# The first part of the last weight, loaded as 112 + 8 + 8 partitions instead of 128

## The chip, the cores and the metric

The kernel runs on one core of one Trainium2 chip. The metric is the device time of one execution in microseconds (us), median over several runs on the same chip. A core has 16 DMA engines that bring data from the far memory (HBM) into 128 partitions of on-chip memory (SBUF). The repeated runs quoted here are all fast: none took over 1.5% more than the fastest run of its kernel.

## The reference, cut to what matters

One decoding step: attention of one token over a cache of 65,536 keys and values in four heads, plus a small mixer network, added together.

```python
x = A_x
xn = _layernorm(x)
return x + _A_ref(xn, A_k_cache, A_v_cache, A_wq, A_wo) + _B_ref(xn, B_w1, B_w2, B_w3, B_w4)
# in _B_ref, the last product, on which the change bears:
h2 = _gelu(_layernorm(x1) @ w3) @ w4        # w4: 3584 x 1024, bf16, 7.3 MB
```

About 170 MB are read for one token, so the kernel is a long stream of loads with a little arithmetic beside it.

## The kernel before

The cache passes through three slots of 64 KB per partition. The last weight, `w4`, is the last thing to be loaded. It has 28 column blocks of 1,024 values per partition and comes in four parts of falling size, so that little tensor work is left when the last part lands. Every part is one transfer over 128 partitions. A partition's piece of the first part is one run of 17 x 2,048 = 34,816 bytes. I call such a piece of one partition a row below. In the code `P` is 128 and `D` is 1,024; `KV` holds the slots, `q_sp` is the queue of the sync engine, and `chan` gives each transfer its semaphore, a counter that tells when data have landed.

```python
def rows_src(w, r0, nrow):
    return w.rearrange("(p r) n -> p (r n)", p=P)[:, r0 * w.shape[1]:(r0 + nrow) * w.shape[1]]
# ...
w4_parts = [(0, 17), (17, 7), (24, 3), (27, 1)]
b_W4 = [_B() for _ in w4_parts]

def w4_dma(i):
    r0, nr = w4_parts[i]
    _dma(q_sp, chan("w4%d" % i), lambda e: e.dma_start(out=KV[:, slot(20), r0 * D:(r0 + nr) * D], in_=rows_src(B_w4, r0, nr)), writes=[b_W4[i]])
# ... in the last pass over the cache, once the last keys have been read out of that slot:
for i in range(len(w4_parts)):
    # (waits for the readers of the slot: cut)
    w4_dma(i)
# ... at the end, one group of matmuls for each part, as it lands:
for i, (r0, nr) in enumerate(w4_parts):
    out_rows([(gh_bf[:, r:r + 1], KV[:, slot(20), r * D:(r + 1) * D]) for r in range(r0, r0 + nr)], [b_W4[i], b_gh], last=(i == len(w4_parts) - 1))
```

## Time and profile before

The median was 401.73 us (401.70 to 402.13).

| what | before |
|---|---|
| span of the profiled run | 400.7 us |
| rate of all DMA engines, mean | 425 GB/s |
| issue of the last weight | 369.5 us |
| last landing of the last weight | 397.8 us |
| one 34,816-byte row on one engine | 1.29 us |

These lines of the page cut the span into 40 slices of 10 us: first the busy share of the 16 DMA engines in tenths, then what they moved.

```profile
DMA  9999899999999999999999999999999999999994
GB/s 419 419 391 486 381 478 445 420 425 419 432 419 446 464 420 425 419 445 419 440 458 420 419 419 458 427 433 445 428 419 419 446 445 414 445 440 432 393 417 195
```

The engines are full (8 or 9 tenths in every slice) up to the last slice at 390 us.

The timeline has the matmuls of the four parts and the final cast: start, busy time, what it is, and in brackets the idle time just before and who ended it.

```profile
391.04 2.03 PE L543 MATMUL S_ps<-KV,gh_bf 128*1 128x256 bf16 x68 [2.74 <-DMA KV<-in_B_w_dram]
395.29 0.93 PE L543 MATMUL S_ps<-KV,gh_bf 128*1 128x256 bf16 x28 [2.22 <-DMA KV<-in_B_w_dram]
397.18 0.81 PE L543 MATMUL S_ps<-KV,gh_bf 128*1 128x256 bf16 x12 [0.96 <-DMA KV<-in_B_w_dram]
398.16 0.38 PE L543 MATMUL S_ps<-KV,gh_bf 128*1 128x256 bf16 x4 [0.16 <-PE S_ps L543]
398.59 0.43 DVE L612 CAST orow<-S_ps 128x256 bf16<-128x256 f32 x1 [15.77 <-PE S_ps L543]
```

Each part's matmuls wait for its landing. The chain of work that ended last says the same for the end as a whole: start, length, what.

```profile
370.37 26.78 DMA KV<-in_B_w_dram
397.18 0.84 PE S_ps L543 x12
```

The page's list of transfers has size and time from issue to landing:

```profile
KV<-in_B_w_dram SPq DMA_DIRECT2D x1, 4352.0 KB, 21.5
KV<-in_B_w_dram SPq DMA_DIRECT2D x1, 1792.0 KB, 25.4
```

The 21.5 us of the first part is mostly queueing: its first row starts at 377.0 us, behind the load ahead of it.

One thing more is read from the trace's own records. It has 16 updates of the semaphore for each part. I take each for the landing of one engine's share, so that they show how far the engines are apart. For the last part they come in three sets: seven engines at 394.6 to 395.3 us, four at 396.3 to 396.5, and five at 397.6 to 397.8. The packet records show how they drift apart. 13 packets of 16,384 bytes are on the queue that the page calls "q8 instruction"; I call them instruction fetches. Each took 1.02 to 1.11 us, and at the end of twelve of them a packet of the stream starts that takes about 0.5 us longer than others of its size (1.79 us instead of 1.29 for the row after the fetch at 381.1 us). The landings of a load spread as the fetches add up: before the first fetch all 16 come within 0.7 us, after one fetch (load landing from 48.2 us on) one of them is 1.9 us behind the first, after nine (338.7 us) nine are 1.5 to 3.2 us behind.

### The profile page before, as it was taken

How to read it: one execution, taken by the hardware profiler on the slowest of the kernel's cores; microseconds unless marked ns; L12 is line 12 of the kernel's file. 1: busy time of each engine (PE TensorE's matmuls, PEld its weight loads, DVE VectorE, ACT ScalarE, POOL GpSimd, SP SyncE). 2: the span in 40 equal slices, each digit the busy share in tenths (PEclk: the TensorE clock that was granted, in tenths of full speed). 3: DMA queues.
4: the chain of work that ended last, by engine and by line, in shares of the span. 5: the costliest groups of instructions: out<-in, count | busy, mean ns of one | idle time of the engine just before them, and what ended most of it. 6: DMA issues, size and time to landing. Idle time of an engine off the chain costs nothing.

```text
span 400.7 us, 3966 instructions
## 1 busy us (share of the span) xinstructions
PE 176.5 (44%) x1611; PEld 70.7 (18%) x1627; DVE 224.5 (56%) x347; ACT 25.2 (6%) x53; POOL 7.1 (2%) x30
## 2 busy tenths in 40 slices
PE   0034767245334513374345342643462335437664
PEld 0022435011011101121111120111121111102242
DVE  0024221985398446763985558659746685696400
ACT  1000000011001100101011001100110011010100
POOL 5000000000000000000000000000000000000000
PEclk9999668556655655555556656555566656555588
DMA  9999899999999999999999999999999999999994
GB/s 419 419 391 486 381 478 445 420 425 419 432 419 446 464 420 425 419 445 419 440 458 420 419 419 458 427 433 445 428 419 419 446 445 414 445 440 432 393 417 195
DMA packets 3770, 170.13 MB, mean 425 GB/s; under 512 B 548, under 2 KB 552, under 8 KB 808
## 3 DMA queue, kind: packets, MB, share of 16 engines
q1 hardware_dynamic: 3608, 169.87, 98.4%
q8 instruction: 13, 0.21, 0.2%
q14 instruction: 5, 0.04, 0.0%
q10 hardware_dynamic: 144, 0.00, 0.0%
HBM read 169.87 MB, written 0.00 MB: 424 GB/s over the span
## 4 chain that ended last, share of the span: by engine, by line
DMA 41%; DVE 30%; PE 23%; issue 3%; another core or an unknown queue 2%; POOL 0%; SPq 0%; ACT 0%; DVEq 0%
DMA KV<-in_A_k_cache_dram 29%; DVE KV L436 21%; PE S_ps L448 8%; DMA KV<-in_B_w_dram 7%; DMA KV<-in_A_x_dram 6%; PE OT_ps L492 5%; PE S_ps L385 3%; DVE pT_f L483 2%; PE M_ps L400 2%; DVE mrow L455 2%; PE S_ps L353 1%; PE M_ps L520 1%; DVE Yall L369 1%; PE PT_ps L479 1%
## 5 line engine op out<-in xcount | busy, mean ns | idle before, releaser
L436 DVE STREAM_TRANSPOSE KV<-KV 128x1024 f32<-128x1024 f32 x128 | 148.6, 1210 | 8.8 <-DMA KV<-in_A_k_cache_dram 8.7
L448 PE MATMUL S_ps<-KV,Yall 128*32 128x512 bf16 x512 | 60.7, 622 | 114.5 <-DVE KV L436 114.5
L492 PE MATMUL OT_ps<-KV,pT_f 128*32 128x512 bf16 x512 | 59.3, 612 | 1.3 <-PE OT_ps L492 1.3
L448 PEld LDWEIGHTS S_ps<-KV,Yall 128*32 128x32 bf16 x512 | 16.8, 125 | 148.0 <-DVE KV L436 132.2
L483 DVE STREAM_TRANSPOSE pT_f<-PT_ps 128x512 f32<-128x512 f32 x32 | 22.6, 706 | 28.2 <-PE S_ps L448 12.0
L470 ACT ACTIVATE p_sb<-S_ps,brun 128x1024 bf16<-128x1024 f32 x16 | 17.8, 1115 | 281.0 <-DVE brun L468 177.3
L455 DVE TENSOR_REDUCE mrow<-S_ps 128x1 f32<-128x1024 f32 x16 | 19.5, 1216 | 16.8 <-PE S_ps L448 16.7
L479 PE MATMUL PT_ps<-p_sb,permR 128*128 128x512 bf16 x16 | 8.8, 553 | 37.2 <-DVE pT_f L483 37.2
L492 PEld LDWEIGHTS OT_ps<-KV,pT_f 128*32 128x32 bf16 x512 | 17.1, 132 | 35.0 <-issue 33.3
L505 DVE SCALAR_TENSOR_TENSOR O_acc<-O_acc,ff,OT_ps 128x512 f32<-128x512 f32 x12 | 8.9, 744 | 23.6 <-PE OT_ps L492 23.6
L385 PE MATMUL S_ps<-KV 128*32 128x512 bf16 x88 | 12.3, 549 | 2.9 <-DVE KV L333 2.9
L458 PE MATMUL M_ps<-Rm,Lmat 128*128 128x16 bf16 x16 | 3.1, 192 | 22.6 <-DVE Rm L456 22.5
L313 DVE CAST KV<-KV 128x8 f32<-128x8 bf16 x1 | 0.2, 171 | 22.3 <-DMA KV<-in_A_x_dram 22.3
L479 PEld LDWEIGHTS PT_ps<-p_sb,permR 128*128 128x128 bf16 x32 | 3.3, 102 | 43.1 <-ACT p_sb L470 15.4
L612 DVE CAST orow<-S_ps 128x256 bf16<-128x256 f32 x1 | 0.4, 426 | 15.8 <-PE S_ps L543 15.8
L400 PE MATMUL M_ps<-ident_f,pT_f 64*128 64x2 f32 (+2 forms) x32 | 7.9, 373 | 2.3 <-DVE pT_f L393 2.3
L400 PEld LDWEIGHTS M_ps<-ident_f,pT_f 64*128 64x128 f32 (+2 forms) x32 | 7.7, 326 | 4.3 <-DVE pT_f L393 4.3
L393 DVE COPY pT_f<-S_ps 64x512 f32<-64x512 f32 (+1 forms) x3 | 2.1, 686 | 11.1 <-PE S_ps L385 11.1
L523 DVE TENSOR_TENSOR cb_R<-M_ps,maskD 32x128 f32<-32x128 f32 x4 | 1.1, 287 | 12.1 <-PE M_ps L520 12.1
L458 PEld LDWEIGHTS M_ps<-Rm,Lmat 128*128 128x128 bf16 x16 | 1.6, 102 | 34.5 <-DVE Rm L456 34.5
L338 PE MATMUL M_ps<-KV 8*128 8x8 bf16 x1 | 0.2, 161 | 16.2 <-DVE Dmat_f L337 16.2
L543 PE MATMUL S_ps<-KV,gh_bf 128*1 128x256 bf16 x112 | 4.2, 290 | 6.1 <-DMA KV<-in_B_w_dram 5.9
(82 smaller groups left out, 95.4 us busy)
## 6 DMA issues: line engine op xcount, KB each, us to landing
KV<-in_B_w_dram SPq DMA_DIRECT2D x1, 7168.0 KB, 48.1
KV<-in_B_w_dram SPq DMA_DIRECT2D x1, 4352.0 KB, 21.5
KV<-in_B_w_dram SPq DMA_DIRECT2D x2, 2048.0 KB, 28.3
KV<-in_B_w_dram SPq DMA_DIRECT2D x1, 1792.0 KB, 25.4
KV<-in_B_w_dram SPq DMA_DIRECT2D x1, 768.0 KB, 26.8
KV<-in_B_w_dram SPq DMA_DIRECT2D x1, 256.0 KB, 27.0
KV<-in_A_k_cache_dram SPq DMA_DIRECT2D x8, 38.9
KV<-in_A_v_cache_dram SPq DMA_DIRECT2D x8, 29.8
```

Source lines behind the costliest of these rows:

```text
L385: fns.append(lambda e, j=j, k=k, mv=mv: e.matmul(S_ps[32 * (k % 4):32 * (k % 4) + 32, bank + k // 4, :], vec[:, j:j + 1].broadcast_to([P, ...
L400: fns.append(lambda e, b=b, nb=nb, c=c: e.matmul(M_ps[:, c0 + 16 * b + c:c0 + 16 * b + 4 * nb:4], pT_f[0:32 * nb, b, c:512:4], ident_f[0:3 ...
L436: _op(q_dve, lambda e, o=o: e.transpose(out=KV32[:, s, o:o + 1024], in_=KV32[:, s, o:o + 1024]), reads=[b_KV[s][4 * sub + ix]], writes=[b_ ...
L448: fns.append(lambda e, we=we, cm=cm, mv=mv: e.matmul(S_ps[32 * cm:32 * cm + 32, n % 4, :], Yall[:, h, we, :, :].rearrange("p a g -> p (a g ...
L455: _op(q_dve, lambda e: e.reduce_max(mrow[:, k:k + 1], S_ps[:, 2 * k:2 * k + 2, :].rearrange("p b c -> p (b c)"), axis=AX.X), reads=b_S[2 * ...
L458: _op(q_pe, lambda e: e.matmul(M_ps[:, 0:16], Lmat[:, :], Rm[:, k, :], start=True, stop=True), reads=[b_R[k], b_const], writes=[b_M])
L470: _op(q_act, lambda e: e.activation(p_sb[:, :, :].rearrange("p b c -> p (b c)"), S_ps[:, 2 * k:2 * k + 2, :].rearrange("p b c -> p (b c)") ...
L479: _op(q_pe, lambda e: e.matmul(PT_ps[:, :], permR[:, :], p_sb[:, n % 2, :], start=True, stop=True), reads=[b_p[n % 2], b_const], writes=[b ...
L483: _op(q_dve, lambda e: e.transpose(out=pT_f[:, n % 2, :], in_=PT_ps[:, :]), reads=[b_PT], writes=[b_pT[n % 2]])
L492: fns.append(lambda e, q=q, q4=q4: e.matmul(OT_ps[32 * q4:32 * q4 + 32, g % 2, :], pT_bf[:, n % 2, q, :, 1], KV[:, s, 8192 * sub + 512 * q ...
L505: _op(q_dve, lambda e: e.scalar_tensor_tensor(out=O_acc[:, 0:512], in0=O_acc[:, 0:512], scalar=ff[:, k:k + 1], in1=OT_ps[:, k, :], op0=ALU ...
L543: fns.append(lambda e, lhs=lhs, rhs=rhs, jj=jj: e.matmul(S_ps[32 * jj:32 * jj + 1, 0, 0:256], lhs, rhs[:, 256 * jj:256 * jj + 256], start= ...
```

## The change

It means to use that difference: give the engines that end early more rows, and the others fewer. The first part is split by partition. 112 partitions are shared out among all 16 engines, seven rows each; two transfers of 8 partitions run on eight engines, one row each. No record numbers the engines. I call the eight that carry a load of 8 partitions engines 0 to 7, and take them to be the same eight for every such load. So eight engines carry nine rows and eight carry seven, where all carried eight.

```diff
         w4_parts = [(0, 17), (17, 7), (24, 3), (27, 1)]
-        b_W4 = [_B() for _ in w4_parts]
+
+        def w4_split(i):
+            return ((0, 112), (112, 120), (120, P)) if i == 0 else ((0, P),)
+
+        b_W4 = [[_B() for _ in w4_split(i)] for i in range(len(w4_parts))]
 
         def w4_dma(i):
             r0, nr = w4_parts[i]
-            _dma(q_sp, chan("w4%d" % i), lambda e: e.dma_start(out=KV[:, slot(20), r0 * D:(r0 + nr) * D], in_=rows_src(B_w4, r0, nr)), writes=[b_W4[i]])
+            for j, (p0, p1) in enumerate(w4_split(i)):
+                _dma(q_sp, chan("w4%d%d" % (i, j)), lambda e, p0=p0, p1=p1: e.dma_start(out=KV[p0:p1, slot(20), r0 * D:(r0 + nr) * D], in_=rows_src(B_w4, r0, nr)[p0:p1]),
+                     writes=[b_W4[i][j]])
# (cut: the two places that wait for a part now wait for all its transfers)
```

The instructions of the tensor, vector, scalar and pool engines stay the same and in the same order; only the sync queue issues two more transfers.

More of the change, by code (lines that the diff above doesn't have):

```diff
@@ L588, in bass_parallel_sum__gqa_block_cached__mixer_s_mlp__decode_kernel @@
                         for sv, vv in list(bk.r.items()) + list(bk.w.items()):
-                            b_W4[i].add_read((sv, vv))
+                            for bw in b_W4[i]:
+                                bw.add_read((sv, vv))
                     w4_dma(i)
@@ L610, in bass_parallel_sum__gqa_block_cached__mixer_s_mlp__decode_kernel @@
         for i, (r0, nr) in enumerate(w4_parts):
-            out_rows([(gh_bf[:, r:r + 1], KV[:, slot(20), r * D:(r + 1) * D]) for r in range(r0, r0 + nr)], [b_W4[i], b_gh], last=(i == len(w4_parts) - 1))
+            out_rows([(gh_bf[:, r:r + 1], KV[:, slot(20), r * D:(r + 1) * D]) for r in range(r0, r0 + nr)], b_W4[i] + [b_gh], last=(i == len(w4_parts) - 1))
         _op(q_dve, lambda e: e.tensor_copy(orow[:, :], OUT), reads=[b_OUT], writes=[b_orow])
```

## The prediction

The cuts take out what no trace showed: how rows are given to engines, and where engines meet when they write. With them go terms of the forecast's sum, which came to +8 to +11 us by a hand model. The +7.7 us in it is an estimate from the measured 1.29 us of a row: four engines that write neighbouring rows were taken to need 4 x 1.29 = 5.2 us, which is 3.9 us more for each of the two 8-partition transfers. This was an assumption, and it is what the 70% is given to. The two humps of the distribution were put near 402 us without it and near 410 to 412 us with it.

> What bounds the kernel. The page's profile shows the 16 DMA engines busy in tenths of 9 in nearly every slice and 425 GB/s over a 400.7 us span, so the kernel is a stream of transfers. At the end (timeline view) the tensor engine has finished everything else at about 388.3 us and only waits for the last weight: matmuls on its four parts start at 391.0, 395.3, 397.2 and 398.2 us. The chain of waits ends with 26.8 us of that weight's transfer, then 0.84 + 0.41 us of matmuls, a 0.43 us cast and the output store. So the end moves one for one with the last landing, at 397.8 us.
>
> How the tail runs. In the trace's packet records a 34,816-byte row of the first part takes 1.29 us (27 GB/s); each engine carries eight of these rows, then 8 x 0.54, 8 x 0.24 and 8 x 0.08 us. The semaphore updates of the last part come in three groups: seven engines at 394.6 to 395.3 us, four at 396.3 to 396.5, five at 397.6 to 397.8. The late ones are engines that were held up earlier by 16 KB instruction fetches: the packet records show a gap of about 1.05 us and about 0.5 us added to the next packet each time. The intent is visible: give engines with slack more rows.
>
> What changes. [...] So eight engines carry nine rows and eight carry seven, +-1.29 us. Two extra issues on the sync queue (0.43 us each, at about 370 us) are hidden: the part's packets start only at 377 us. Matmul, vector and scalar work is unchanged.
>
> If that were all: nine of 16 engines are not early, so not all can sit among the eight relieved. The end then moves by about -0.1 us (a middle engine gains a row) to +1.3 us (a late one does).
>
> What I expect beside it. [...] My estimate from 1.29 us: [...] +7.7 us on engines with nine rows, on top of the added row, less up to 1-2 us of slack; the 112-row transfer, seven consecutive rows per engine, may collide a little too. [...] I give it about 70%.
>
> Predicted: 409.5 us, range 401.3 to 413.5; faster by over 2% 0.01, within 2% 0.45, slower by over 2% 0.54. The distribution has two humps[...].
>
> What would show it. Right: 34,816-byte packets of the two 8-partition transfers lasting 3 to 5 us instead of 1.29; first part landing 8 or more us later; DMA GB/s falling in the last slices; the other eight engines landing early; the wait of the tensor engine on the last weight growing by the same amount; everything before 377 us unchanged. If the packets stay at 1.29 us, [...] only the one-row shift remains. Also wrong if the 112-partition transfer uses another distribution of rows[...].

## More of the kernel before

The next view has the busy time of each engine in stretches near the end; its last two columns are the DMA engines' busy share and GB/s.

```profile
core 0: us, PE busy (x) PEld busy (x) DVE busy (x) ACT busy (x) POOL busy (x), PEclk, DMA share, GB/s
370.00:380.00 10.00, 6.49 (x112) 2.68 (x105) 4.47 (x11) 1.30 (x3) 0.00 (x0) 0.52 0.94 406
380.00:390.00 10.00, 6.58 (x138) 4.76 (x138) 1.29 (x5) 0.00 (x0) 0.00 (x0) 0.83 0.97 413
390.00:400.00 10.00, 4.15 (x112) 2.44 (x112) 0.43 (x1) 0.00 (x0) 0.00 (x0) 0.84 0.56 228
```

## The result, and the profile after

The median was 419.5 us (418.66 to 420.48), against 401.76 us on the same chip: 1.044 times as long, 95% interval 1.0416 to 1.0465. A ratio here is the mean time of one kernel's fast runs over that of the other's of the same rounds, so it is not quite the ratio of the medians.

The page's slices of the changed kernel, 10.5 us each here:

```profile
DMA  9999899999999999999999999999999999999983
GB/s 400 400 488 438 377 489 406 406 483 406 413 477 406 419 471 406 425 464 401 438 463 396 444 450 403 450 438 409 456 426 419 446 425 431 439 413 230 179 147 155
```

The engines look just as busy, but in the last four slices they move 147 to 230 GB/s. An engine can be busy and move little: a row took 2.3 to 4.6 us instead of 1.29 (medians, below). The stretches of time, in the same columns as before:

```profile
370.00:380.00 10.00, 6.49 (x112) 2.53 (x105) 4.55 (x11) 1.29 (x3) 0.00 (x0) 0.55 1.08 371
380.00:390.00 10.00, 4.97 (x137) 3.72 (x136) 1.29 (x5) 0.00 (x0) 0.00 (x0) 1.00 0.94 214
390.00:400.00 10.00, 0.00 (x0) 0.00 (x0) 0.00 (x0) 0.00 (x0) 0.00 (x0) 0.63 1.12 173
400.00:410.00 10.00, 0.00 (x0) 0.00 (x0) 0.00 (x0) 0.00 (x0) 0.00 (x0) 0.50 0.78 174
```

From 380 us on, with the transfers of the first part under way, the rate is about half or less of the 413 GB/s before. From 390 to 410 us no compute engine does anything. The timeline's tail, the chain and the transfers:

```profile
410.33 3.36 PE L549 MATMUL S_ps<-KV,gh_bf 128*1 128x256 bf16 x68 [20.83 <-DMA KV<-in_B_w_dram]
414.17 0.94 PE L549 MATMUL S_ps<-KV,gh_bf 128*1 128x256 bf16 x28 [0.48 <-DMA KV<-in_B_w_dram]
416.06 0.50 PE L549 MATMUL S_ps<-KV,gh_bf 128*1 128x256 bf16 x12 [0.96 <-DMA KV<-in_B_w_dram]
416.73 0.28 PE L549 MATMUL S_ps<-KV,gh_bf 128*1 128x256 bf16 x4 [0.16 <-DMA KV<-in_B_w_dram]
```

```profile
371.57 45.09 DMA KV<-in_B_w_dram
416.73 0.31 PE S_ps L549 x4
```

```profile
KV<-in_B_w_dram SPq DMA_DIRECT2D x1, 3808.0 KB, 35.7
KV<-in_B_w_dram SPq DMA_DIRECT2D x1, 1792.0 KB, 43.4
```

The tensor engine's idle time before the first part went from 2.74 to 20.83 us, and the end moved with the last landing, from 397.8 to 416.7 us. The 112-partition transfer alone, with 7/8 of the bytes, now takes 35.7 us from issue to landing instead of 21.5.

The trace's packet records say where in the part it happens. They list each row with its start and length; here are the medians of every sixteen rows of the first part, in order of start, in us:

```
before   1.29  1.30  1.29  1.29  1.29  1.30  1.29  1.29
after    2.64  2.46  2.36  2.56  2.32  2.55  4.02  4.58
```

Two things are wrong at once. The 112-partition rows are all nearly twice as slow, from the first on: no row of the first part took under 1.96 us. The rows of the 8-partition transfers, which fall mostly into the last two figures, take three times as long and more.

### The profile page after: what moved, and what is told of

The parts are those of the page before. It is cut to its first block, busy times and chain, and to the rows that moved or that the text cites. A ratio compares the mean times of both kernels' runs of the same rounds, so it can differ in the third digit from the quotient of the medians.

```text
span 419.2 us, 3969 instructions
## 1 busy us (share of the span) xinstructions
PE 175.0 (42%) x1611; PEld 69.9 (17%) x1627; DVE 224.5 (54%) x347; ACT 25.2 (6%) x53; POOL 7.1 (2%) x30
## 4 chain that ended last, share of the span: by engine, by line
DMA 44%; DVE 29%; PE 22%; issue 3%; another core or an unknown queue 2%; SPq 0%; POOL 0%; ACT 0%; DVEq 0%
DMA KV<-in_A_k_cache_dram 28%; DVE KV L436 20%; DMA KV<-in_B_w_dram 11%; PE S_ps L448 8%; DMA KV<-in_A_x_dram 5%; PE OT_ps L492 5%; PE S_ps L385 3%; DVE pT_f L483 2%; PE M_ps L400 2%; DVE mrow L455 1%; PE S_ps L353 1%; PE M_ps L520 1%; DVE Yall L369 1%; DVE pT_f L393 0%
## 5 line engine op out<-in xcount | busy, mean ns | idle before, releaser
L549 PE MATMUL S_ps<-KV,gh_bf 128*1 128x256 bf16 x112 | 5.1, 339 | 22.4 <-DMA KV<-in_B_w_dram 22.4
L549 PEld LDWEIGHTS S_ps<-KV,gh_bf 128*1 128x1 bf16 x112 | 2.9, 102 | 24.7 <-issue 21.1
## 6 DMA issues: line engine op xcount, KB each, us to landing
KV<-in_B_w_dram SPq DMA_DIRECT2D x1, 3808.0 KB, 35.7
```

What stands on the lines that cost most here:

```text
L549: fns.append(lambda e, lhs=lhs, rhs=rhs, jj=jj: e.matmul(S_ps[32 * jj:32 * jj + 1, 0, 0:256], lhs, rhs[:, 256 * jj:256 * jj + 256], start= ...
```

## The experiments

The theories were these. **S**: engines that write rows of one group at the same time slow each other. What a group is, is assumption: four neighbouring rows and the four that lie 32 further on, so 0 to 3 with 32 to 35, and 64 to 67 with 96 to 99. Not every group was tested; these loads of 64 KB rows bear it out, each given with its whole time. In the second kernel of isolated loads (lines 631 and 639 to 642 of its sync queue) rows 0 and 4 took 5.0 us and the eight rows 0, 4, ... 28 took 5.1, but rows 0 and 1 took 6.6, rows 0 and 32 took 7.5, and rows 0 to 3 took 11.2. In the third (line 629) ten rows at a step of 12, no two of one group, took 5.3. **U**: the uneven share, nine rows against seven, is the cost. **H**: the reading side is the cost. **N**: a row is slow if another engine writes it than in the 128-partition form. Three more came up on the way. **C**: an engine that is slowed in a shared group also holds back engines that share none. **K**: something that only 16 engines together meet. **X**: a general limit for engines that write other rows than those of the 128-partition form.

In the recorded expectations, too, the passages on where engines meet are cut. The time that stands right behind a cut at the end of two of them, 9.0 and 419.5 us, is for the case that S plays no part.

### All engines even again, the odd transfers kept

```diff
-            return ((0, 112), (112, 120), (120, P)) if i == 0 else ((0, P),)
+            return ((0, 112), (112, P)) if i == 0 else ((0, P),)
```

> The changed kernel with its two transfers of 8 partitions made one of 16 partitions, so that all 16 engines carry eight rows again, as before. Theory U (the uneven share, nine rows against seven, is the cost): the time goes back to about 402 us. Theory S[...]: the 112-row transfer keeps its 2.45 us a row, which costs 7 x 1.16 = 8.1 us over before; the 16 rows [...] 5.2 us instead of 1.29, so 3.9 us more: about 402 + 12 = 414 us, between 411 and 416.

It took 417.87 us, 1.040 times before. With eight rows on every engine again the loss is nearly all still there, so U falls as the main cause. S had said 411 to 416, so it is too small as sized. The tensor engine's wait for the first part stays nearly as long as in the changed kernel (20.83 us):

```profile
407.67 3.80 PE L549 MATMUL S_ps<-KV,gh_bf 128*1 128x256 bf16 x68 [17.81 <-DMA KV<-in_B_w_dram]
```

### Isolated loads of 34,816-byte rows

Lines were added behind the end of the kernel before. Each waits for the one ahead:

```diff
         q_sp.wait(ev_out)
+        for q in (q_pe, q_dve, q_act, q_pool):
+            q_sp.wait((q.sem, q.cnt))
+        WP = B_w4.rearrange("(p r) n -> p (r n)", p=P)
+        def probe(fn):
+            q_sp.wait(_dma(q_sp, chan("probe"), fn))
+        N = 17 * D
+        probe(lambda e: e.dma_start(out=KV[0:128, 0, 0:N], in_=WP[0:128, 0:N]))
+        probe(lambda e: e.dma_start(out=KV[0:112, 0, 0:N], in_=WP[0:112, 0:N]))
# ... fifteen more
```

> The kernel before with 17 isolated loads added after its output; each waits for the one ahead, a row is 34,816 bytes. The order: 128 rows; 112 from row 0; 112 from row 16; 96; 64; 32; 16; 16 rows at a step of 4; 16 at a step of 8; 16 at a step of 7; 8 rows 112 to 119; 8 at a step of 4 from row 0; the same from row 64; 4 neighbouring rows; 4 at a step of 4; rows 112 to 119 filled from source rows 0, 4, ... 28; rows 0, 4, ... 28 filled from source rows 112 to 119. Theory S[...]: a row takes 1.29 us[...] (128 rows; 8 at a step of 4, from 0 and from 64; 4 at a step of 4), 5.2 us for 4, 8 or 16 neighbouring rows[...], 2.6 us for 16 at steps of 4 and 8, 1.3 to 2.6 at a step of 7; the last two go by the destination: 5.2, then 1.29 us. Theory H (neighbouring source rows collide in the far memory): the last two go by the source. Theory N[...]: 8 rows at a step of 4 are fast from row 0 but slow from row 64. For 112 rows S with seven neighbouring rows per engine expects 10 to 13 us in all; the changed kernel's trace had about 2.45 us a row, so I expect about 17 us unless the rest of the program plays a part.

The timeline of the sync queue for this kernel: start of an issue, its length, source line. As each waits for the one ahead, the distance between two starts is the whole time of a load. Lines 625, 626 and 627 are 128 rows, 112, and 112 from row 16; 635, 636 and 637 are rows 112 to 119, 8 rows at a step of 4 from row 0, and the same from 64; 640 and 641 are the two with exchanged sources.

```profile
400.83 0.34 SPq L625 DMA_DIRECT2D KV<-in_B_w_dram  x1
413.66 0.34 SPq L626 DMA_DIRECT2D KV<-in_B_w_dram  x1
430.99 0.32 SPq L627 DMA_DIRECT2D KV<-in_B_w_dram  x1
...
509.94 0.28 SPq L635 DMA_DIRECT2D KV<-in_B_w_dram  x1
516.32 0.70 SPq L636 DMA_DIRECT2D KV<-in_B_w_dram  x1
520.19 0.64 SPq L637 DMA_DIRECT2D KV<-in_B_w_dram  x1
...
534.23 0.28 SPq L640 DMA_DIRECT2D KV<-in_B_w_dram  x1
540.63 0.65 SPq L641 DMA_DIRECT2D KV<-in_B_w_dram  x1
```

The 128 rows need 413.66 - 400.83 = 12.8 us, and 112 rows, with fewer bytes, 17.3 us. Eight neighbouring rows need 6.4 us, eight at a step of 4 need 3.9. From the packet records, with the rate from the first start to the last end of a load:

| destination | rows per group at a time | one row, median us | GB/s |
|---|---|---|---|
| 128 rows | 1 | 1.29 | 387 |
| 112 rows | 1 or 2 | 2.19 | 250 |
| 96 rows | 1 or 2 | 2.56 | 213 |
| 64 rows / 32 rows | 2 | 2.74 / 2.71 | 191 / 183 |
| 16 rows | 4 | 3.89 | 111 |
| rows 112 to 119 | 4 | 3.69 | 65 |
| 8 rows, step 4, from 0 / from 64 | 1 | 1.84 / 1.89 | 134 / 137 |
| rows 112-119, from sources 0, 4, ... 28 | 4 | 3.75 | 63 |
| rows 0, 4, ... 28, from sources 112-119 | 1 | 1.84 | 144 |

The first row of a load carries about 0.55 us of start (1.84 us against 1.29), so 1.84 is the quick figure for a load of one row per engine. The time goes by the destination whatever the source: H falls. Rows from 64 on are as quick as from 0 (1.89 and 1.84 us): N falls, if the same eight engines carry both. Four of one group were 3.7 to 3.9 us instead of the 5.2 expected. And 112 rows came out slower than S allows if engines act independently. That was left to explain. (Not in the table: 16 rows at steps of 4, 8 and 7 had medians of 2.26, 2.42 and 2.01 us, and 112 rows from row 16 took 18.1 us.)

### The pair of 8-partition loads by itself

Added to the kernel before, between the first part and the rest (data unused; the result stays right):

```diff
+        q_sp.wait((q_pe.sem, q_pe.cnt))
+        for rows in (slice(112, 120), slice(120, P)):          # the partner: slice(0, 32, 4), slice(1, 32, 4)
+            ev_extra = _dma(q_sp, chan("extra"), lambda e, rows=rows: e.dma_start(out=KV[rows, slot(18), 0:17 * D], in_=rows_src(B_w4, 0, 17)[rows]))
+        for i in (1, 2, 3):
+            w4_dma(i)
# (cut: before this only the first part is issued; at the end the sync queue waits for the added loads too)
```

> The kernel before, all its transfers as they were, plus two loads of 8 rows of 34,816 bytes whose data nobody uses, for partitions 112 to 119 and 120 to 127, queued between the last weight's first part and the rest. They cost by themselves what the pair costs in the changed kernel. Theory S:[...] about 4.6 us a row as in the changed kernel's trace, 9.2 us; engines 0 to 7 hold two of the late ones, so the end moves by nearly all of it: 410 to 412 us. Theory U (it is the extra bytes on half of the engines): 2 x 1.29 = 2.6 us, 404.4 us, the same as its partner e_plus8s.

> The same two loads with the same bytes on the same eight engines, but for partitions 0, 4, ... 28 and 1, 5, ... 29[...]. Theory S: 1.29 us a row, about +2.6 us, 403.5 to 405 us. If the source side, the unevenness or the number of transfers were the cost, it would be as slow as e_plus8.

Times: 412.81 us for the neighbouring rows, 404.55 us for those at a step of 4; 401.85 before. The same bytes on the same engines cost 11.0 us in one arrangement and 2.7 us in the other. So 412.81 - 404.55 = 8.3 us is the price of shared groups for this pair. The 2.7 us are two rows of 1.29 us and show that the engines used here include some that end last. The timelines' lines for the first two parts, with neighbouring rows and then with a step of 4:

```profile
397.83 3.80 PE L543 MATMUL S_ps<-KV,gh_bf 128*1 128x256 bf16 x68 [11.94 <-DMA KV<-in_B_w_dram]
405.70 1.66 PE L543 MATMUL S_ps<-KV,gh_bf 128*1 128x256 bf16 x28 [4.07 <-DMA KV<-in_B_w_dram]
```

```profile
391.18 3.79 PE L543 MATMUL S_ps<-KV,gh_bf 128*1 128x256 bf16 x68 [4.50 <-DMA KV<-in_B_w_dram]
397.65 1.66 PE L543 MATMUL S_ps<-KV,gh_bf 128*1 128x256 bf16 x28 [2.68 <-DMA KV<-in_B_w_dram]
```

Most of the price falls on the first part, which is queued ahead of the pair: it landed at 397.8 us instead of 391.1. I read this so: engines that are done with it start on the pair, and those that are not are then slowed.

### The 112-partition load by itself

Built likewise: one unused load of 112 partitions of 34,816 bytes, or one of 128 partitions of 30,464 bytes, which is the same number of bytes.

```diff
+        ev_extra = _dma(q_sp, chan("extra"), lambda e: e.dma_start(out=KV[0:112, slot(18), 0:17 * D], in_=rows_src(B_w4, 0, 17)[0:112]))
# the partner:
+        ev_extra = _dma(q_sp, chan("extra"), lambda e: e.dma_start(out=KV[:, slot(18), 0:119 * 128], in_=B_w4.rearrange("(p r) n -> p (r n)", p=P)[:, 0:119 * 128]))
```

> The kernel before, plus one load of 112 partitions of 34,816 bytes whose data nobody uses, queued between the last weight's first part and the rest: the changed kernel's large transfer alone, all 16 engines carrying the same. If [...] (theory C, as the isolated loads with pairs did), a row takes about 2.4 us here too and the end moves by 7 x 2.4 = 16 to 17.5 us: 418 to 420 us, 7 to 8 us more than its partner e_plus128. With independent engines[...]: 11.6 us, 413.5 us. [...] 9.0 us, as its partner.

> The partner: the same bytes as one load of 128 partitions of 30,464 bytes (seven eighths of a row)[...]. 3.9 MB at 27 GB/s and engine is 9.0 us: 410 to 411.5 us under every theory.

Times: 422.61 us and 411.36 us. The timelines' lines for the second part's matmuls, which wait behind the added load, first with 112 partitions, then with 128:

```profile
415.65 1.66 PE L543 MATMUL S_ps<-KV,gh_bf 128*1 128x256 bf16 x28 [17.86 <-DMA KV<-in_B_w_dram]
```

```profile
404.60 1.66 PE L543 MATMUL S_ps<-KV,gh_bf 128*1 128x256 bf16 x28 [11.20 <-DMA KV<-in_B_w_dram]
```

For the same bytes the 112-partition form costs 422.61 - 411.36 = 11.3 us more, beyond the 7 to 8 expected. A row took the 2.4 us expected and a little more (medians 2.41 to 2.62 by sixteens); but the first part, queued ahead, also landed later, at 394.05 us instead of 391.32. This is the larger part of the loss, and it has nothing to do with an uneven share: all 16 engines carry seven rows.

### Why all 112 rows are slow: three more kernels of isolated loads

They hold loads of 64 KB rows, built as above. In the load of 128 rows such a row takes 2.42 us; as the first row of a load, with the start, about 3.0 us.

> The kernel before, with a mark (64 bytes to 8 partitions at a step of 4[...]) queued behind the last weight, and after the output 14 isolated loads of 64 KB rows: 128 rows; 8 at a step of 4; 8 at a step of 5[...]; 8 at a step of 2[...]; rows 112 to 119; 16 at a step of 7; 112 rows; 112 rows as seven transfers of 16 at a step of 7; rows 112 to 119 and 120 to 127 together; 4 neighbours; 2 neighbours; rows 0 and 32; rows 0 and 4; 1 row. Mark: its eight landings show whether engines 0 to 7 are those that fall behind by instruction fetches. Theory S with independent engines: a row alone 2.42 us; step of 5: two rows of 4.84 us, six of 2.42; step of 2: 4.84; rows 112 to 119: 9.7; 2 neighbours and rows 0 and 32: 4.84; rows 0 and 4: 2.42; the two eights together 19.4 us. Rival C (a blocked engine also holds back others): at a step of 5 and 7 the rows [...] take clearly over 2.42 us too; this would explain why all rows of the 112-row load were slow[...]. If 112 rows are given out as blocks of seven neighbours, the one transfer and the seven take the same time, about 7 x 4.2 us.

> The kernel before with 14 isolated loads of 64 KB rows after the output, to find why all 16 rows at a step of 7 took near 4.3 us[...]. Order: 128 rows; 14 rows at a step of 9[...]; 8 rows at a step of 9; 10 at a step of 9; 12 at a step of 9; 10 at a step of 12[...]; 16 at a step of 7; the same filled from source rows 0 to 15; the same filled from source rows 0, 8, ... 120; 14 at a step of 9 filled from source rows 0 to 13; 14 neighbouring rows; 8 at a step of 4 from 0; the same from 64; 14 at a step of 9 again. Theory S with independent engines: 3.0 us (2.42 and 0.55 of start) [...] for all 14 at a step of 9. Rival X[...]: 14 rows at a step of 9 take 4 us or more, 8 rows stay at 3.0, 10 and 12 lie between. Rival H (source side): the three at a step of 7 differ by source.

> The kernel before with 15 isolated loads of 64 KB rows after the output, to find what makes all rows of a 16-engine load slow[...]. Order: 128 rows; 10, 12, 14, 15, 16 rows at a step of 7 (one row per engine[...]); 14 at a step of 9 (no pair); 98 rows and 112 rows in sequence (seven per engine on 14 and on 16 engines); 8, 10, 12, 14, 16 rows at a step of 5 (one, three, four, five, five pairs); 70 rows (seven per engine, ten engines). Theory S with independent engines: in the step-of-7 loads four rows take 4.8 to 5.4 us and the others 3.0, at any count of engines; 98 and 112 rows take 21.8 us by my hand model. Rival C (a blocked engine holds back others): the lone rows get slower step by step with more engines or more pairs. Rival K (something only 16 engines together meet): 15 rows at a step of 7 still have 11 quick rows, 16 have none; 98 rows take about 22 us and 112 rows about 31.

From the packet records (a pair is two rows of the load, one per engine, of one group):

| load, one row per engine | engines | pairs | rows, us |
|---|---|---|---|
| 8 rows, step 9 | 8 | 0 | 2.72 to 3.29 |
| 14 rows, step 9 (three loads) | 14 | 0 | 2.42 to 3.75, medians 3.10 to 3.15 |
| 8 rows, step 5 (fourth kernel) | 8 | 1 | two of 4.60, six of 2.77 to 3.32 |
| 10 rows, step 5 | 10 | 3 | 4.16 to 5.21 |
| 10 rows, step 7 | 10 | 2 | 3.72 to 4.57 |
| 14 rows, step 7 | 14 | 2 | 3.81 to 4.67 |
| 16 rows, step 7 | 16 | 2 | 4.07 to 5.05 |
| the same, sources 0 to 15 / 0, 8, ... 120 | 16 | 2 | 4.07 to 4.94 / 3.90 to 5.06 |

For a few of these loads, the fourth kernel's sync queue (again the distance of two starts is the whole time): 10 rows at a step of 7 (line 625), 14 at a step of 9 (630), 98 rows (631), 112 rows (632) and 8 rows at a step of 5 (633):

```profile
422.37 0.84 SPq L625 DMA_DIRECT2D KV<-in_A_k_cache_dram  x1
429.66 0.74 SPq L626 DMA_DIRECT2D KV<-in_A_k_cache_dram  x1
...
459.31 0.78 SPq L630 DMA_DIRECT2D KV<-in_A_k_cache_dram  x1
465.06 0.36 SPq L631 DMA_DIRECT2D KV<-in_A_k_cache_dram  x1
491.71 0.32 SPq L632 DMA_DIRECT2D KV<-in_A_k_cache_dram  x1
524.30 0.67 SPq L633 DMA_DIRECT2D KV<-in_A_k_cache_dram  x1
531.44 0.73 SPq L634 DMA_DIRECT2D KV<-in_A_k_cache_dram  x1
```

Fourteen engines without a pair stay quick (medians 3.10 to 3.15 us), so X falls. Ten engines with two pairs are slow throughout, so K falls for these loads. The source changes little, so H falls here too. With one pair only the two rows of the pair are slow. With two pairs or more, rows that share no group are slow as well (no row of the ten at a step of 7 took under 3.72 us). That is C in its outcome, and as a step rather than the slow growth I had described: with one pair in the load six of eight rows stay at 2.77 to 3.32 us, with two pairs all are slow. The effect is weaker in a single shorter row: 16 rows of 34,816 bytes at a step of 7, two pairs too, had a median of 2.01 us, against 1.84 without a pair.

How the 112 rows are given out was tested by the second kernel. One transfer of 112 rows and seven transfers of 16 rows at a step of 7, which repeat "seven neighbours to each engine" by hand, are lines 636 and 637 in its sync queue:

```profile
460.65 0.33 SPq L636 DMA_DIRECT2D KV<-in_A_k_cache_dram  x1
493.21 4.32 SPq L637 DMA_DIRECT2D KV<-in_A_k_cache_dram  x7
526.85 0.62 SPq L638 DMA_DIRECT2D KV<-in_A_k_cache_dram  x2
```

The two take 32.6 and 33.6 us, as blocks of seven neighbours would have it. The two 8-partition loads together (line 638 to the next issue at 546.70) took 19.9 us, of which their packets fill 18.0, where four per group had been put at 19.4.

In that layout engine e writes partition 7e + i in step i, and the groups give the number of pairs in each step. The fourth kernel has 98 rows too, the same blocks of seven on 14 engines. Pairs by step, and the median of the step's rows from the packet records, in us:

```
step                  0     1     2     3     4     5     6
98 rows, pairs        2     1     1     1     1     1     1
98 rows, median     4.39  3.10  3.39  2.86  2.92  2.93  3.52
112 rows, pairs       2     2     2     1     1     2     2
112 rows, median    4.10  4.76  4.78  3.39  3.53  4.68  4.65
```

Steps with two pairs are slow for all engines, steps with one pair are much quicker, in both loads. (I take the engines to keep step with each other; how far they drift apart inside these loads was not measured.) This rule, which came from the loads of one row per engine, so tells 98 rows (25.2 us) from 112 (31.2 us). It was put together after these runs, and no further run was made to test it. Three loads that it was not made from can be held against it. Two agree: 96 rows, with two or three pairs in every step, have no step under a median of 2.19 us; 70 rows, with four or five pairs in every step, have none under 4.86. (The 70 rows ran on 14 engines with five rows each, by their 14 landings, not on ten with seven as I had expected.) 112 rows from row 16, with one pair in steps 2 and 3 alone, agree in half: their medians are 1.99, 2.20, 1.77, 2.33, 2.14, 2.45 and 2.24 us. Inside a kernel the rule is not seen: steps 3 and 4 of the changed kernel (2.56, 2.32) and of the 112-partition load by itself (2.62, 2.41) are no quicker than the others. There the engines begin a load several us apart: in the changed kernel their shares of the load ahead landed between 377.4 and 384.0 us.

### Two rows per group instead of four

```diff
-            return ((0, 112), (112, 120), (120, P)) if i == 0 else ((0, P),)
+            return ((0, 112, 1), (112, P, 2), (113, P, 2)) if i == 0 else ((0, P, 1),)
# and p0:p1 becomes p0:p1:st on both sides
```

> The changed kernel with its two transfers of 8 partitions interleaved: 112, 114, ... 126 and 113, 115, ... 127[...]; rows, bytes and engines are the same, the result is right. Theory S: 2.6 us a row instead of the 4.0 to 4.6 of the changed kernel's trace, so about 2 x 1.7 = 3.5 us faster than the change: 415 to 417 us. [...] 419.5 us as the change.

It took 419.12 us, no better than the change (1.042 times before, against 1.044 for the change in its own rounds). The wait for the first part is again almost that of the changed kernel:

```profile
409.26 3.79 PE L549 MATMUL S_ps<-KV,gh_bf 128*1 128x256 bf16 x68 [18.67 <-DMA KV<-in_B_w_dram]
```

The last 32 rows as a whole did become shorter: medians by eights between 2.7 and 3.9 us instead of 3.5 to 4.6. But those on the path that ends last did not. In the changed kernel the last landings of 112, 8, 8 and the second part come 2.3, 2.5 and 4.1 us apart. I read that as one engine that reaches its two extra rows last, when few others are left in its groups; the records do not name the engine of a packet. With the step of 2 the distances are 2.7, 2.5 and 4.1 us. The prediction of 415 to 417 us had charged the mean row to the last engine.

### The same shift of bytes, nearly without shared groups

The first part as a 128-partition transfer that is shorter by n of 17 column blocks; the n blocks come as sixteen 8-partition transfers at a step of 4, so on engines 0 to 7 with a group each. n = 2 is nearly the change's shift (32.8 KB against 34.8), n = 1 half of it.

```diff
+            wide = nr - SHIFT if i == 0 else nr
+            # the 128-partition transfer takes `wide` column blocks; then, for i == 0:
+                for j in range(16):
+                    sel_ = slice(32 * (j // 4) + j % 4, 32 * (j // 4) + 32, 4)
+                    _dma(q_sp, chan("w4s%d" % j), lambda e, sel_=sel_: e.dma_start(out=KV[sel_, slot(20), (r0 + wide) * D:(r0 + nr) * D], in_=rows_src(B_w4, r0 + wide, SHIFT)[sel_]), writes=[b_W4[i][1 + j]])
```

> The kernel before, with the share moved as the change intended (engines 0 to 7 get nine ninths of a row more, engines 8 to 15 as much less, 32.8 KB)[...]: 15 of the first part's 17 column blocks come as one transfer of 128 partitions, the last two as sixteen transfers of 8 partitions at a step of 4 (4 KB each, engines 0 to 7). Theory S[...]: no loss like the change's; engines 0 to 7 end 1.2 us later, 8 to 15 1.2 us earlier. If engines 0 to 7 are the early ones the end moves between -1.2 and +0.2 us, if the late ones it moves by +1.2 us: 400.5 to 403.3 us. Theory U (uneven share, or many transfers on half of the engines, is the cost): over 410 us.

> The same with half the shift, 16.4 KB (one column block in sixteen transfers of 2 KB rows): engines 0 to 7 end 0.6 us later, 8 to 15 0.6 us earlier. If 0 to 7 are the early ones -0.6 us against before (about 401.2 us), else +0.6 us. Theory U: half of its loss, over 405 us.

Times: 406.13 us (n = 2) and 404.80 us (n = 1), against 401.83. Neither gains, and both lie above what S allowed. The landings explain most of it. On the latest of engines 0 to 7 the fifteen distances between the sixteen small transfers add up to 4.5 us with 4 KB rows and 3.1 us with 2 KB rows, that is 0.30 and 0.21 us each. At 27 GB/s the bytes need 0.15 and 0.08 us. So 2.3 and 2.0 us (my differences) are beyond the bytes of the small transfers; what takes them was not shown. Then there is the shift itself, 1.2 and 0.6 us. Together this is 3.5 and 2.6 us of the 4.3 and 3.0 lost; the rest stays unexplained.

Whether the intent could have worked is told by the mark in the second kernel of isolated loads: 64 bytes to eight partitions, queued behind the last part. Its eight landings lie about 0.2 us behind those of the engines that carried it: five belong to the early set, one to the middle set, two to the late set. So the eight engines that got more rows include two of the latest.

## Why the prediction was wrong

- **What bounds the end: right.** The last landing moved by 18.9 us in the profiled runs, whose spans differ by 18.5, and the median time by 17.7 us. The issue of the weight began at 369.5 and 369.6 us. One thing earlier did change: the load ahead of the first part, still under way when its rows began, landed at 384.0 us instead of 380.6.
- **The two 8-partition transfers: the cause right, the size partly by luck.** I had +7.7 us; the pair by itself cost 8.3 us more than the same bytes with a group for each engine. Rows of 3 to 5 us were seen, and the 70% given to this term was the right side. But a row took less than the 5.2 us of the estimate (medians 3.0 and 4.3 us in the last two sixteens of rows of the run with the pair alone), and by the last landings 6.6 of the 8.3 us are a delay of the transfer ahead, which I had not counted. In the changed kernel the last landings of the two transfers follow at 2.3 and 2.5 us, only 2.2 us over two plain rows together, and two rows per group in place of four changed the time by no more than the noise.
- **The uneven share: it fits, but was not measured alone.** "to +1.3 us (a late one does)": two of the late engines are among the eight that got more, and two plain rows cost 2.7 us, so one costs about 1.3. With even shares (and one transfer of 16 partitions for the pair) the kernel was 1.6 us quicker, 417.87 against 419.5.
- **The step that failed: the 112-partition transfer.** This term of the sum was mis-sized. The prediction put it as "the 112-row transfer, seven consecutive rows per engine, may collide a little too". The layout was right, the size was not. By itself it cost 11.3 us more than the same bytes over 128 partitions, the largest term. My hand model of queues and groups let every engine run on at full rate unless its own group was shared. It gives 21.8 us for 112 rows of 64 KB; measured were 31.2 us. The isolated loads show instead that from two pairs on, engines that share no group are slow too (3.72 to 4.57 us for all of ten engines); in the kernel the 112 rows had medians of 2.3 to 2.6 us from the first on, where the model has a row at 1.29 us unless its own group is shared.
- **The sum.** The pieces measured alone, 11.3 + 8.3 + 1.3 = 20.9 us, exceed the 17.7 us of the whole. They do not simply add up, because a transfer with shared groups also slows the one ahead of it (by 3.4, 6.6 and 2.7 us in the changed kernel, with the pair alone and with the 112 partitions alone). The last landings of the changed kernel divide its 18.9 us in another way: the 112-partition transfer lands at 405.3 us, 15.6 us later than seven plain rows would have (391.0 - 1.3); the two extra rows add 2.2 us over plain ones, the ninth row itself 1.3, and the second part takes 0.2 us less. How much of the 15.6 us is the doing of the pair behind it was not measured.
- **"The other eight engines landing early": wrong.** The earliest final landing came at 410.6 us, against 394.6 us before. All engines had lost time in the 112-partition transfer.
- **Open.** By what path two pairs hold back the rest while one pair does not. No run shows it.

No version tried beats the kernel before.

## What to carry to other kernels

Keep large loads at all 128 partitions: as isolated loads of 34,816-byte rows these moved at 387 GB/s, against 250 for 112 and 213 for 96 partitions. To cut one into pieces, cut along the columns, so that each piece still spans the 128 partitions: in the kernel 3.9 MB over 128 partitions added 9.5 us, the same bytes over 112 added 20.8 (411.36 and 422.61 against 401.85). "It runs on 16 engines" is not enough: the 96- and 112-partition loads moved more slowly than the 128-partition load although every engine had work. An engine that looks busy may move little (a share of 1.12 at 173 GB/s in the changed kernel), so read the GB/s beside the busy share. Before shifting work to idle engines, check by a marked transfer which engines are really early: of the eight that got more rows here, two were among the latest.
